# Reordering the first loads of a fused S5 + SwiGLU kernel: w1 of the first two gate tiles on both queues behind chunks 0 and 1 of x, chunk 3 of x behind w3

## The chip, the cores and the metric

The kernel runs on one core of a Trainium2 chip. Times are device microseconds (us) of that core, and the metric is the time of one execution. A "span" is the time from the first to the last instruction of a profiled execution; it is some 2 us shorter than the timed execution.

Engine names: PE is TensorE's matmuls, PEld its weight loads, DVE is VectorE, ACT is ScalarE, POOL is GpSimd, SP is SyncE. A q behind a name (SPq) is that engine's instruction sequencer.

## The reference

A layer norm of x (2048 tokens of 512 features) feeds a state-space layer (part A) and a SwiGLU block (part B). Both are added to x. Cut to what matters here:

```python
def _B_ref(x, w1, w3, w2):                      # w1, w3: 512 x 1792
    gate = jnp.einsum("bsd,df->bsf", x, w1)
    up = jnp.einsum("bsd,df->bsf", x, w3)
    h = _silu(gate) * up
    return jnp.einsum("bsf,fd->bsd", h, w2)

x = A_x
xn = _layernorm(x, axis=-1)
return x + _A_ref(xn, ...) + _B_ref(xn, B_w1, B_w3, B_w2)
```

## The kernel before

The kernel takes tokens in four blocks of 512, each of four chunks of 128. TensorE can begin its real work when chunk 0 of x has landed, been normalized and transposed, and the first columns of w1 have landed. The head of the program issues its first transfers for that; `nc.sync` and `nc.scalar` are the two engines that issue.

```python
    def load_w(f0, f1, eng1=nc.sync, eng3=nc.sync):
        eng1.dma_start(out=w1_sb[:, :, f0:f1], in_=w1v[:, :, f0:f1])
        eng3.dma_start(out=w3_sb[:, :, f0:f1], in_=w3v[:, :, f0:f1])

    for c in range(2):                      # chunks 0 and 1: a half on each queue
        for eng, dsl in ((nc.sync, slice(0, D // 2)), (nc.scalar, slice(D // 2, D))):
            eng.dma_start(out=x_blk[0][:, c, dsl], in_=xv[:, c, dsl])
    nc.scalar.dma_start(out=x_blk[0][:, 3, :], in_=xv[:, 3, :])
    nc.sync.dma_start(out=x_blk[0][:, 2, :], in_=xv[:, 2, :])
    load_w(0, 2 * P)                        # first w1, first w3: 256 KB each
    load_w(2 * P, 4 * P)                    # second w1, second w3
    # ... cut: bulk_loads() issues the rest, after a wait for ScalarE
```

The first weights are used here. `quarter` multiplies one chunk of tokens with some gate tiles, first with w1, then with w3:

```python
            def quarter(cl, fs, parts=1):
                tsl = slice(cl * P, (cl + 1) * P)
                n = NDT // parts
                for side, w in ((0, w1_sb), (1, w3_sb)):
                    for i in range(0, NDT, n):
                        for f in fs:
                            for dt in range(i, i + n):
                                nc.tensor.matmul(...)      # 128 columns
            # ... cut: chunks 0 and 1 are normalized and transposed
            ln_stats(0, 2)                  # VectorE: statistics of chunk 2
            ln_first_rstd(2)
            ln_stats(0, 3)                  # VectorE: statistics of chunk 3
            ln_first_rstd(3)
            ln_apply(0, 2)                  # VectorE: only now is chunk 2 normalized
            ln_apply(0, 3)
            quarter(0, (0, 1), 2)           # 8 matmuls with w1, then 8 with w3
            quarter(1, (0, 1))              # again, for chunk 1
            # ... cut
            ln_first_transpose(2)
            quarter(0, (2,))                # third tile: second w1, second w3
            ln_first_transpose(3)
```

Note the order on VectorE: chunk 2 is normalized after the statistics of chunk 3, so the transposes of chunk 2 wait for the landing of chunk 3.

Of the kernel before, what the change touches and what calls it, by code (L numbers as in the profile page):

```python
# [17 lines left out]
P = 128  # L18
# [45 lines left out]
def kernel(  # L64
# [17 lines left out]
    nc = tc.nc  # L82
# [26 lines left out]
    xv = A_x[0].rearrange("(c p) d -> p c d", p=P)  # L109
# [15 lines left out]
    w1_sb = const.tile([P, NDT, F], BF16, name="w1_sb")  # L125
    w3_sb = const.tile([P, NDT, F], BF16, name="w3_sb")
# [24 lines left out]
    x_blk = [x_all[:, i] for i in range(NBLK)]  # L151
    w1v = B_w1.rearrange("(t p) f -> p t f", p=P)
    w3v = B_w3.rearrange("(t p) f -> p t f", p=P)
# [4 lines that stand above are left out]
# [6 lines left out]
    for c in range(2):  # L164
        for eng, dsl in ((nc.sync, slice(0, D // 2)), (nc.scalar, slice(D // 2, D))):
            eng.dma_start(out=x_blk[0][:, c, dsl], in_=xv[:, c, dsl])
    nc.scalar.dma_start(out=x_blk[0][:, 3, :], in_=xv[:, 3, :])
    nc.sync.dma_start(out=x_blk[0][:, 2, :], in_=xv[:, 2, :])
    load_w(0, 2 * P)
    load_w(2 * P, 4 * P)  # L170

    def bulk_loads():
# [1111 lines left out]
```

## Time and profile before

| | before |
|---|---|
| timed runs, beside the changed kernel | 200.99, 200.81, 201.39, 201.04 us, median 201.01 |
| profiled span | 198.9 us |
| first w3: issued, landed | 2.59, 6.64 us |
| second w3: landed | 8.62 us |
| start of the last matmul to end of span | 2.98 us |

"Landed" is when the last of the 16 DMA engines that share a transfer has finished it. Read such a kernel as a full engine (TensorE) with a head in front of it and a tail behind: only a hole in TensorE's stream, a later start, or a longer tail moves the end. The prediction below shows the lines of the head (waits: who waits, for whom: us in all, times, longest).

```profile
SPq L1279 <- DMA out_dram<-xn: 1.0, 3, 0.5
```

```profile
196.53 0.36 ACTq L1072 DMA_DIRECT2D out_dram<-xn  x1
```

The last store is issued at 196.53, and the span ends 198.9 − 196.53 = 2.4 us later. In between SyncE waits three times for stores.

### The profile page before, as it was taken

The page shows a single profiled execution, that of the slowest core. Times are in us where ns is not written, and L with a number is a line of the kernel's source. Part 1 is how long each engine was busy: PE and PEld are TensorE (multiplying, and loading weights), DVE is VectorE, ACT ScalarE, POOL GpSimd, SP SyncE. Part 2 cuts the span into 40 slices and gives each one's busy share as a digit, 9 for nine tenths or more (in the row PEclk, how much of TensorE's full clock was granted, in tenths as well). Part 3 has the DMA queues.
Part 4 walks back from the last instruction along what each step waited for, and adds up shares of the span by engine and source line. Part 5 has one row for each costly group of instructions (what it writes and reads, how often), then busy time and mean ns, then how long its engine had stood idle before and what let it go on. Part 6 is the DMA issues. An engine that isn't in the chain of part 4 may idle for free.

```text
span 198.9 us, 3703 instructions
## 1 busy us (share of the span) xinstructions
PE 195.2 (98%) x1401; PEld 130.7 (66%) x1401; DVE 182.2 (92%) x257; ACT 135.0 (68%) x281; POOL 50.9 (26%) x75
## 2 busy tenths in 40 slices
PE   8999999999999999999999999999999999999994
PEld 2874444444444488856555478888566678888893
DVE  3699699999999999989999997999999999999972
ACT  4899797799999987968998684362688782111220
POOL 7170289700411134041202305040021303300000
PEclk9999999999999999999999999999999999999999
DMA  5999999992497054730997546838147723941111
GB/s 154 319 240 185 328 200 98 348 280 46 70 181 141 0 105 82 135 106 0 164 154 107 100 83 108 169 84 124 53 64 134 143 52 57 170 96 33 53 40 44
DMA packets 32258, 25.12 MB, mean 126 GB/s; under 512 B 16240, under 2 KB 29936, under 8 KB 32240
## 3 DMA queue, kind: packets, MB, share of 16 engines
q0 software_dynamic: 6128, 11.38, 33.6%
q1 hardware_dynamic: 25536, 13.21, 28.2%
q10 hardware_dynamic: 576, 0.30, 0.5%
q8 instruction: 11, 0.18, 0.4%
q14 instruction: 7, 0.06, 0.1%
HBM read 7.74 MB, written 2.10 MB: 49 GB/s over the span
## 4 chain that ended last, share of the span: by engine, by line
PE 96%; DMA 1%; DVE 1%; issue 0%
PE gu_ps L587 34%; PE gu_ps L1055 18%; PE y_ps L1055 10%; PE gu_ps L849 7%; PE bu_ps L1055 7%; PE y_ps L454 3%; PE bu_ps L454 3%; PE y_ps L870 3%; PE y_ps L781 3%; PE gu_ps L619 2%; PE gu_ps L781 2%; PE bu_ps L781 1%; PE bu_ps L870 1%; DMA x_blk<-in_A_x_dram 1%; PE bu_ps L619 1%; PE y_ps L243 1%
## 5 line engine op out<-in xcount | busy, mean ns | idle before, releaser
L587 PE MATMUL gu_ps<-xnT,w_sb 128*128 128x512 bf16 x312 | 69.6, 379 | 0.0
L587 PEld LDWEIGHTS <-w_sb 128*128 128x128 bf16 x312 | 30.5, 98 | 34.2
L1055 PEld LDWEIGHTS <-act 128*128 128x128 f16 x462 | 43.5, 98 | 5.4
L596 ACT ACTIVATE g<-gu_ps 128x512 bf16<-128x512 f32 x41 | 24.8, 606 | 5.9 <-PE gu_ps L587 3.5
L597 ACT ACTIVATE u<-gu_ps 128x512 bf16<-128x512 f32 x41 | 24.9, 606 | 4.4 <-PE gu_ps L587 4.1
L505 DVE TENSOR_TENSOR_SCAN u<-rho,ends,u 128x512 bf16<-128x512 f32 x16 | 20.0, 1271 | 0.0
L527 POOL DMA_DIRECT2D act<-p x7 | 9.2, 1321 | 34.1 <-DVE act L519 22.1
L1055 PE MATMUL gu_ps<-w_sb,act 128*128 128x256 bf16 (+3 forms) x126 | 16.0, 267 | 0.0
L849 PE MATMUL gu_ps<-xnT,w_sb 128*128 128x512 bf16 x64 | 15.9, 379 | 0.0
L604 DVE TENSOR_TENSOR act<-g,u 128x1024 f16<-128x1024 bf16 x21 | 14.3, 680 | 0.0
L861 ACT ACTIVATE g<-gu_ps 128x512 bf16<-128x512 f32 x14 | 8.4, 599 | 5.4 <-PE gu_ps L849 5.0
L454 PEld LDWEIGHTS <-bt 128*128 128x128 bf16 x64 | 6.3, 98 | 7.5
L1078 ACT ACTIVATE x_blk<-gu_ps 128x256 f32<-128x256 f32 (+1 forms) x9 | 3.3, 368 | 10.6 <-PE gu_ps L1055 10.6
L1055 PE MATMUL bu_ps<-w_sb,act 128*128 128x256 bf16 (+3 forms) x84 | 10.4, 264 | 0.0
L1055 PE MATMUL gu_ps<-ct,act 128*128 128x256 f16 (+1 forms) x72 | 10.4, 267 | 0.0
L849 PEld LDWEIGHTS <-w_sb 128*128 128x128 bf16 x64 | 6.3, 98 | 4.8
L505 DVE TENSOR_TENSOR_SCAN u<-rho,u 128x512 bf16<-128x512 f32 x8 | 9.2, 1207 | 0.0
L1055 PEld LDWEIGHTS <-x_blk 128*128 128x128 f16 x88 | 8.6, 98 | 1.0
L1055 PEld LDWEIGHTS <-tw 128*128 128x128 f16 x88 | 8.6, 98 | 1.0
L513 DVE TENSOR_TENSOR p<-u,tabe 128x2048 f16<-128x2048 bf16 (+1 forms) x8 | 8.7, 1086 | 0.1
L519 DVE TENSOR_TENSOR act<-u,tabe 128x2048 f16<-128x2048 bf16 (+1 forms) x8 | 8.7, 1085 | 0.0
L488 DVE TENSOR_TENSOR u<-u,tabe 128x2048 bf16<-128x2048 bf16 x7 | 8.5, 1220 | 0.1
(203 smaller groups left out, 392.5 us busy)
## 6 DMA issues: line engine op xcount, KB each, us to landing
act<-p POOLq DMA_DIRECT2D x6, 512.0 KB, 6.1
xn<-x_blk POOLq DMA_DIRECT2D x4, 512.0 KB, 5.5
out_dram<-xn SPq DMA_DIRECT2D x15, 128.0 KB, 1.7
w_sb<-in_B_w_dram SPq DMA_DIRECT2D x1, 1792.0 KB, 8.2
act<-act POOLq DMA_DIRECT2D x5, 352.0 KB, 4.6
w_sb<-in_B_w_dram SPq DMA_DIRECT2D x2, 768.0 KB, 6.1
u<-p POOLq DMA_DIRECT2D x3, 512.0 KB, 5.2
w_sb<-in_B_w_dram SPq DMA_DIRECT2D x4, 256.0 KB, 4.4
```

Of the source, the lines that this page charges most:

```text
L454: nc.tensor.matmul(out=ps, lhsT=bt[:, ri, dt, pt * P:(pt + 1) * P], rhs=xnT_blk[b][:, dt, :], start=(dt == 0), stop=(dt == NDT - 1))
L505: nc.vector.tensor_tensor_scan(out=v, data0=rho[:, pt:pt + 1].to_broadcast([P, TBLK]), data1=v, initial=init, op0=ALU.mult, op1=ALU.add)
L513: nc.vector.tensor_tensor(out=by_state(st["p16"][:, csl]), in0=by_chunk(st["g"][:, :, ::-1, tsl]), in1=by_chunk(tabe[:, psl, 2:0:-1, tsl]) ...
L519: nc.vector.tensor_tensor(out=by_state(act_state(b, hf)[:, csl]), in0=by_chunk(st["g"][:, :, :, tsl]), in1=by_chunk(tabe[:, psl, 0:1, tsl] ...
L527: gp.dma_start(out=a, in_=p16, accum_op=ALU.add)
L587: nc.tensor.matmul(out=ps[:, tsl], lhsT=w[:, dt, f * P:(f + 1) * P], rhs=xnT[:, dt, tsl], start=(dt == 0), stop=(dt == NDT - 1))
L596: nc.scalar.activation(out=g16[:, f % 2, :], in_=g_ps, func=ACT.Silu)
L597: nc.scalar.activation(out=u16[:, f % 2, :], in_=u_ps, func=ACT.Copy)
L604: nc.vector.tensor_tensor(out=act_gates(b, f - 1), in0=split(g16), in1=split(u16), op=ALU.mult)
L781: nc.tensor.matmul(out=out[:, h * TH:(h + 1) * TH], lhsT=left[:, h, k, :], rhs=right[:, k, :], start=(start and h == 0 and k == 0), stop=( ...
L849: nc.tensor.matmul(out=ps, lhsT=w[:, dt, f * P:(f + 1) * P], rhs=xnT[:, dt, :], start=(dt == 0), stop=(dt == NDT - 1))
L1055: nc.tensor.matmul(out=out, lhsT=left[:, k, :], rhs=right[k][:, cols], start=(start and k == 0), stop=(k == NK - 1), skip_group_check=True)
```

## The change

The intent: w1 of the first two gate tiles is wanted first, so half of it goes on each queue directly behind chunks 0 and 1 of x. Chunk 3 of x isn't wanted soon, so it goes behind w3.

```diff
-    nc.scalar.dma_start(out=x_blk[0][:, 3, :], in_=xv[:, 3, :])
+    for eng, k in ((nc.sync, 0), (nc.scalar, 2)):
+        eng.dma_start(out=w1_sb[:, k:k + 2, 0:2 * P], in_=w1v[:, k:k + 2, 0:2 * P])
     nc.sync.dma_start(out=x_blk[0][:, 2, :], in_=xv[:, 2, :])
-    load_w(0, 2 * P)
+    nc.sync.dma_start(out=w3_sb[:, :, 0:2 * P], in_=w3v[:, :, 0:2 * P])
+    nc.sync.dma_start(out=x_blk[0][:, 3, :], in_=xv[:, 3, :])
     load_w(2 * P, 4 * P)
```

Bytes are the same. The number of transfers rises by one, as w1 is now two.

## The prediction

> **What bounds the kernel now.** I read the page's first two parts first, to see whether there is an engine whose waits decide the end.
>
> ```profile
> PE 195.2 (98%) x1401; PEld 130.7 (66%) x1401; DVE 182.2 (92%) x257; ACT 135.0 (68%) x281; POOL 50.9 (26%) x75
> ...
> PE   8999999999999999999999999999999999999994
> ...
> DMA  5999999992497054730997546838147723941111
> ```
>
> TensorE (PE) is busy in every slice; only the first and the last are not full. The DMA engines are saturated in the first 40 us as well. So the end is the sum of the TensorE's work plus its few holes, and a change of loads can pay only through a hole. The list of waits for the TensorE has two entries, both before its real work:
>
> ```profile
> PE bu_ps L196 <- PEq L1268: 0.8, 1, 0.8
> PE y_ps L243 <- DVE xn L224: 0.2, 1, 0.2
> ```
>
> No wait for a weight is there, so I went on to the chain that ended last, in order of time, for the head (start, length, what):
>
> ```profile
> 0.73 2.39 DMA x_blk<-in_A_x_dram
> ...
> 3.14 0.70 DVE stats L219
> ...
> 6.32 1.88 PE gu_ps L619 x32
> 8.21 0.11 PE y_ps L315
> 8.31 0.33 PE y_ps L243 x4
> 8.64 0.45 PE bu_ps L619 x8
> ...
> 12.44 8.63 PE gu_ps L587 x40
> ```
>
> The head is: x chunk 0 lands (3.1 us), VectorE statistics, transposes, then the first gate tiles (L619, matmuls of 128 columns) from 6.2 us and no pause after. Eight of them take 0.45 us, 0.056 each. Thirty-two should take 1.79, and took 1.88: there is a hole of about 0.09 us in the first block, too small for the list of waits. The timeline of the weight loads (start, length, what) in three neighbouring windows finds it:
>
> ```profile
> 6.11 0.43 PEld L619 LDWEIGHTS <-w_sb 128*128 128x128 bf16 x7
> 6.44 0.15 PEld L619 LDWEIGHTS <-w_sb 128*128 128x128 bf16 x2
> 6.69 1.29 PEld L619 LDWEIGHTS <-w_sb 128*128 128x128 bf16 x23
> ```
>
> Loads 1 to 8 (the first two tiles' w1) run every 0.056 us from 6.11; the eighth starts at 6.50. The ninth, the first of w3, starts at 6.69 instead of 6.55. When did the transfers land? The timeline gives the issue, the view of one line's transfers the time to landing: w1 2.11 + 3.6 = 5.7; w3 2.59 + 4.1 = 6.7. So **w1 is 0.4 us early, w3 is what is late**, by 0.13 us at the load and, as matmul 9 could otherwise have started 0.056 after matmul 8 (6.55) and started at 6.69, by 0.08 us in the stream.
>
> The same reading for the third tile (f = 2), whose weights come with the next two transfers, issued 3.14 and 3.69, landing after 4.7 and 4.9: 7.8 and 8.6. The loads:
>
> ```profile
> 8.43 0.27 PEld L619 LDWEIGHTS <-w_sb 128*128 128x128 bf16 x4
> 8.67 0.14 PEld L619 LDWEIGHTS <-w_sb 128*128 128x128 bf16 x2
> ```
>
> Loads 1 to 4 (w1) start 8.43 to 8.59; the fifth (w3) would follow at 8.65, and came at 8.67. This second w3 transfer lands at the very moment when it is wanted. There is no slack behind it. After that, matmul starts follow one another by columns and clock to the end of the kernel; I found no other hole above 0.03 us.
>
> **What the Trainium skill says.** (1) "DMA: Bandwidth & Descriptors", section "Issuing engines are not separate DMA queues": transfers issued by ScalarE and SyncE run on the same 16 DMA engines, and spreading them saves only issue time. Here an issue takes 0.37 to 0.51 us on SyncE and the engines are over 100% busy from 4 to 12 us (windows view, DMA share 1.01 to 1.11), so the trace agrees: what counts is the bytes ahead of a transfer. (2) The same page, "Queues, rings and completion order": each DMA engine takes turns between the queues that have work, and a queue's descriptors are consumed in ring order. The landings of before (x 2 and 3 at 4.9 and 5.1, then 5.7, 6.7, 7.8, 8.6) are in order of issue, so I count bytes in issue order. (3) "TensorE: Matmul & The Clock Gate", "Wait — 56ns, not 53.3ns?": warm matmuls follow each other after columns / 2.4 GHz plus about 2.5 ns, 55.6 and 215.7 ns for 128 and 512 columns. The chain agrees: 8.63 / 40 = 0.216 us.
>
> **The change, part by part.** The order on TensorE, VectorE, ScalarE's compute and POOL is the same; only the loads move: ScalarE's queue gets half of w1 for chunk 3 of x, SyncE's gets half of w1, x 2, w3, x 3, and one issue more in all. No byte is added. Landings before, by cumulative KB: 512 at 5.1, 768 at 5.7, 1024 at 6.7, 1280 at 7.8, 1536 at 8.6. By those (an estimate):
>
> - w1, both halves, at 512 KB: 5.1 instead of 5.7. Wanted at 6.11. It had 0.4 us to spare; worth nothing.
> - x 2 at 640 KB: about 5.4 instead of 4.9. VectorE takes it at 5.78: hidden.
> - w3 at 896 KB: about 6.2 instead of 6.7. Wanted at 6.55: the hole closes, **-0.08 us**.
> - x 3 at 1024 KB: about 6.7 instead of 5.1. VectorE wanted it at 6.60, so the statistics of chunk 3 slip by 0.1 us, and with them both normalizations behind them (chunk 2's ends at 7.82 + 0.1, chunk 3's at 8.49 + 0.1). The transposes want them at 8.24 and 8.87, or 0.08 earlier if the hole closes: 0.24 and 0.2 us to spare. Hidden.
> - The loads of tiles 2 and 3: the extra issue pushes theirs from 3.14 and 3.69 to about 3.6 and 4.2, but the engines are a backlog of over 2 us behind by then (1024 KB issued by 3.6 land at 6.7), so landings stay at 7.8 and 8.6. TensorE now arrives 0.08 us earlier and waits for this second w3: **+0.08 us**.
> - SyncE is done with its issues by about 4.7; the next waits for ScalarE and went at 4.94 anyway.
>
> Sum: -0.08 + 0.08 = 0. The hole moves from the first w3 to the second. Even the whole hole is 0.04% of 201 us.
>
> **The rivals.** (a) *The second w3 lands early enough too*: then the 0.08 us stay, 200.9 us. For it: the landing at 8.6 is read only to 0.1 us, and w1 now shares two queues. Against: bytes ahead of it are the same. (b) *x 3 becomes the bound*: if it lands later than about 7.0, transposes of chunk 2, then the whole stream, wait one for one. For it: it goes from 1.5 us early to 0.1 us late. Against: it would have to be 0.3 us later than its bytes say; 0.3 us too late would give 201.2 to 201.3. (c) *The later issue of the second w3 shows*: its issue is 0.5 us later; if half of that reached the landing, TensorE would wait some 0.25 us, 201.2. Against: the saturated engines. (d) *Chunks 0 and 1 are slowed by the smaller pieces of w1 behind them* (512-byte rows in place of 1 KB): chunk 0 is the start of the chain, so each 0.1 us would count in full. Against: chunk 0 landed at 3.1, little more than 1 us after the next transfers were issued, and ring order puts them behind. (e) A gain above 0.2 us would need TensorE to start its gate tiles sooner, but the transposes ahead of them hang on x 0, VectorE and ScalarE, which the change leaves alone.
>
> **Range and chances.** I take 201.0, the median of before. The mechanisms move it by -0.1 to +0.3; the three runs of before spread from 200.81 to 201.39, so the scatter is as large. Range 200.6 to 201.5. Two per cent is 4 us, more than fifty times the hole: faster 0.01, within 0.98, slower 0.01.
>
> **What would show it right or wrong.** Right: in the changed profile the ninth L619-type weight load follows the eighth after 0.056 us; the first w3 lands near 6.2, x 3 near 6.7; the fifth load of the third tile then stands 0.1 us late, just after the second w3's landing at 8.6; the x512 stream starts at the same time as before (12.28) within 0.1. Wrong: a hole before the transposes of chunk 2 or 3 (rival b), the second w3 landing at 8.8 or later (c), chunk 0's statistics starting later than 3.14 (d), or a stream that starts by over 0.2 us sooner, which I have no source for.

## More of the kernel before

"L621" is a line of the kernel; a change in the head shifts the numbers by up to three lines, so L619 of the kernel before is L621 of the changed one.

From the start of the last matmul to the end of the span it is 2.98 us. Results of block 0 are held and stored later; the last stores of the last block are issued by SyncE and ScalarE, and the program then ends in instructions that the kernel doesn't write: waits for its transfers. The waits of SyncE's sequencer (who waits, for whom: us in all, times, longest) and the timeline (start, length, what) of the kernel before show both.

```python
    for cl, o in held:                      # 4 stores of 128 KB
        nc.sync.dma_start(out=ov[:, cl, :], in_=o)
```

## The result, and the profile after

The changed kernel takes 201.93 us (median; 201.83, 201.91, 202.40, 201.94), the kernel before 201.01 beside it. The ratio is 1.0048, with a 95% interval of 1.0026 to 1.0069. Ratios here are the mean time of one kernel's fast runs over that of the other's of the same rounds, so not quite the ratio of the medians quoted. The change is well within 2%, but it is a real loss of about 0.9 us, and 201.93 lies outside the range of 200.6 to 201.5.

The page of the changed kernel, its span, engine totals and the slices of TensorE and of the DMA engines:

```profile
span 200.1 us, 3704 instructions
...
PE 195.1 (98%) x1401; PEld 130.7 (65%) x1401; DVE 182.2 (91%) x257; ACT 134.9 (67%) x281; POOL 50.5 (25%) x75
...
PE   7899999999999999999999999999999999999993
...
DMA  5999999990498054730997446838147723940201
```

TensorE does the same work in the same time (195.1 against 195.2), with one digit less in the first slice and in the last. So the loss sits in the head and in the tail. The waits of TensorE have a new entry, for a weight:

```profile
PE bu_ps L198 <- PEq L1270: 0.8, 1, 0.8
PE gu_ps L621 <- DMA w_sb<-in_B_w_dram: 0.6, 1, 0.6
PE y_ps L245 <- DVE xn L226: 0.3, 1, 0.3
```

The timeline of the changed kernel (start, length, what; in brackets the idle time before and what ended it) places it:

```profile
5.96 0.49 PEld L621 LDWEIGHTS <-w_sb 128*128 128x128 bf16 x8
7.20 1.34 PEld L621 LDWEIGHTS <-w_sb 128*128 128x128 bf16 x24 [0.75 <-DMA w_sb<-in_B_w_dram]
7.62 0.69 DVE L221 BATCH_NORM_STATS2 stats<-x_blk 128x6 f32<-128x512 bf16 x1 [1.08 <-DMA x_blk<-in_A_x_dram]
```

The eight loads of w1 run from 5.96, some 0.15 us earlier than before. The ninth, the first of w3, comes at 7.20, after 0.75 us in which no weight was loaded, just after the first w3 has landed (7.16). VectorE's statistics of chunk 3 begin at 7.62, when chunk 3 has landed. The view of one line's transfers tells the way of the first w3 (issue time and, last, issue to landing), here before and then after:

```profile
L157 SPq DMA_DIRECT2D w_sb<-in_B_w_dram x1: 507/507/507, 2.6 to 2.6; - x1
...
DMA to landing us min/median/max: 4.1/4.1/4.1
```

```profile
L170 SPq DMA_DIRECT2D w_sb<-in_B_w_dram x1: 434/434/434, 2.6 to 2.6; - x1
...
DMA to landing us min/median/max: 4.5/4.5/4.5
```

It is issued at nearly the same time (2.62 instead of 2.59) with fewer bytes ahead of it, and lands 7.16 − 6.64 = 0.5 us later. The chain that ended last passes through chunk 3 of x in the changed kernel:

```profile
3.10 4.49 DMA x_blk<-in_A_x_dram
...
7.62 0.71 DVE stats L221
...
8.53 0.31 DVE xn L226
8.89 0.40 PE y_ps L245 x4
9.28 0.45 PE bu_ps L621 x8
...
13.12 8.63 PE gu_ps L589 x40
```

The stream of 512-column matmuls starts 13.12 − 12.44 = 0.68 us later than before. Step by step: the ninth load is 7.20 − 6.69 = 0.51 later than before; chunk 2's transposes, which wait for chunk 3's statistics to let VectorE go on, load at 8.88 instead of 8.24, which is 0.64 later; the rest, 0.04, comes behind. The 0.51 and the 0.64 are not a sum. The transposes follow chunk 3, as the chain shows, and would have stood at 8.88 even if the first w3 had landed in time. So in this profile the wait that ends last is that for chunk 3 of x, and the hole before w3 is hidden in front of it. With chunk 3 in time the late w3 would still have cost about the 0.51 by itself. The last matmul begins at 196.64 instead of 195.95, 0.69 later: nothing is lost or won between. Then the tail. The last store's issue in the timeline, and SyncE's waits, after:

```profile
197.22 0.36 ACTq L1074 DMA_DIRECT2D out_dram<-xn  x1
```

```profile
SPq L1281 <- DMA out_dram<-xn: 1.4, 1, 1.4
```

SyncE waits for stores once, for 1.4 us, instead of three times. From the start of the last matmul to the end it is now 3.42 instead of 2.98 us, 0.44 longer. Head 0.69 and tail 0.44 are 1.13 us, and the unrounded spans differ by 1.12. The profiled pair is thus accounted for in full; its head is above what the timed runs lose on the mean, as the experiments show.

### The profile page after: what moved, and what is told of

Read it like the earlier page. It is cut to its first block, busy times and chain, and to the rows that moved or that the text cites. A ratio compares the mean times of both kernels' runs of the same rounds, so it can differ in the third digit from the quotient of the medians.

```text
span 200.1 us, 3704 instructions
## 1 busy us (share of the span) xinstructions
PE 195.1 (98%) x1401; PEld 130.7 (65%) x1401; DVE 182.2 (91%) x257; ACT 134.9 (67%) x281; POOL 50.5 (25%) x75
## 4 chain that ended last, share of the span: by engine, by line
PE 94%; DMA 2%; SPq 1%; DVE 1%; issue 0%
PE gu_ps L589 34%; PE gu_ps L1057 17%; PE y_ps L1057 10%; PE gu_ps L851 7%; PE bu_ps L1057 7%; PE bu_ps L456 3%; PE y_ps L456 3%; PE y_ps L872 3%; PE y_ps L783 3%; DMA x_blk<-in_A_x_dram 2%; PE gu_ps L783 2%; PE bu_ps L783 1%; PE bu_ps L872 1%; PE bu_ps L621 1%; PE gu_ps L621 1%; SPq L166 0%
## 5 line engine op out<-in xcount | busy, mean ns | idle before, releaser
L221 DVE BATCH_NORM_STATS2 stats<-x_blk 128x6 f32<-128x512 bf16 x8 | 5.4, 681 | 4.1 <-DMA x_blk<-in_A_x_dram 4.1
```

## The experiments

Kernels of one call share a chip and the runs of the kernel before. All outputs were correct. Each diff is against the kernel before unless it says otherwise; where a run only writes `load_w(0, 2 * P)` out as its two transfers, or adds an `assert`, the diff shown leaves that out. A "hole" is the time without a weight load before the ninth load, and a "tail" the time from the start of the last matmul to the end of the span. At first I looked for the whole loss in the head. My theory was that w1 in two halves sets the 16 DMA engines apart, so that the w3 behind it waits for the slowest; rivals were the place of chunk 3 and later issues.

### First call: is it real, and which part?

**after_again**, the changed kernel unchanged:

> The changed kernel once more, to see whether its late w3 is of the order of loads or of one profile. Theory A (the new order makes one DMA engine fall behind in the first w3 transfer; three of four w1-split suspects are tested beside this run): w3 lands at 6.9 us or later, the TensorE hole before the ninth weight load is 0.5 us or more, time 201.7 to 202.2. Theory C (a slow engine of that one profile, the time difference has another cause): w3 lands at 6.2 to 6.6, no hole, and yet about 201.9.

Measured: 202.02 us beside 200.83, ratio 1.0051 [1.0027, 1.0076]. First w3 landed at 7.11. The timeline of the weight loads shows the same hole:

```profile
7.16 0.90 PEld L621 LDWEIGHTS <-w_sb 128*128 128x128 bf16 x16 [0.68 <-DMA w_sb<-in_B_w_dram]
```

The loss repeats.

**x3_behind**, only chunk 3 moved behind w3:

```diff
-    nc.scalar.dma_start(out=x_blk[0][:, 3, :], in_=xv[:, 3, :])
     nc.sync.dma_start(out=x_blk[0][:, 2, :], in_=xv[:, 2, :])
     load_w(0, 2 * P)
+    nc.sync.dma_start(out=x_blk[0][:, 3, :], in_=xv[:, 3, :])
```

> Chunk 3 of x behind w3 on the same queue, w1 whole and in its old place, nothing else. Theory A1 (splitting w1 over both queues sets the engines apart): w3 lands at 6.2 to 6.6, x 3 by 6.9, no hole above 0.1 us, time 200.9 to 201.1. Theory A2 (x 3 behind w3, so that SyncE's queue carries everything, is what costs): w3 at 6.9 or later or x 3 at 7.4 or later, hole 0.3 us or more in sum, time 201.5 to 202.0.

Measured: 201.14, ratio 1.0007 [0.9988, 1.0026]. First w3 landed at 6.51, without a hole before it:

```profile
6.06 1.83 PEld L620 LDWEIGHTS <-w_sb 128*128 128x128 bf16 x32
```

Chunk 3 landed at 7.28, and TensorE waited about 0.46 us for the normalized chunk 2 in the profile, as its list of waits says too:

```profile
PE y_ps L244 <- DVE xn L225: 0.4, 1, 0.4
```

The transposes of chunk 2 load at 8.56 instead of 8.24, and the last matmul begins at 196.35 instead of 195.95, with w3 in time: the late chunk 3 alone delays the stream in this profile. In time, this part alone can't be told from nothing. But the kernel before took 200.78 to 200.89 in five runs and 201.40 and 201.43 in two, and this one 201.05 to 201.25 in all four, so the mean of the kernel before holds slower executions of its own.

**w1_split**, only the halves of w1, chunk 3 where it was but behind ScalarE's half:

```diff
+    for eng, k in ((nc.sync, 0), (nc.scalar, 2)):
+        eng.dma_start(out=w1_sb[:, k:k + 2, 0:2 * P], in_=w1v[:, k:k + 2, 0:2 * P])
     nc.scalar.dma_start(out=x_blk[0][:, 3, :], in_=xv[:, 3, :])
     nc.sync.dma_start(out=x_blk[0][:, 2, :], in_=xv[:, 2, :])
-    load_w(0, 2 * P)
+    nc.sync.dma_start(out=w3_sb[:, :, 0:2 * P], in_=w3v[:, :, 0:2 * P])
```

> w1 of the first two tiles in halves on both queues, chunk 3 of x stays on ScalarE's queue behind its half, not behind w3. Theory A1 (the split sets the engines apart): w3 lands at 6.9 or later, hole 0.4 us or more, time 201.5 or more. Theory A2 (x 3 behind w3 costs): w3 about 6.5, x 3 about 5.6, time 200.9 to 201.1.

Measured: 202.25, ratio 1.0056 [1.0034, 1.0079]. In its profile chunk 0 landed some 0.5 us late and w3, the ninth transfer, was issued only at 3.61: it waits for the semaphore of an earlier transfer, a half of chunk 0, that landed at 3.59. It landed at 7.67.

**x3_ahead**, the changed kernel with chunk 3 ahead of w3 (diff against the changed kernel):

```diff
+    nc.sync.dma_start(out=x_blk[0][:, 3, :], in_=xv[:, 3, :])
     nc.sync.dma_start(out=w3_sb[:, :, 0:2 * P], in_=w3v[:, :, 0:2 * P])
-    nc.sync.dma_start(out=x_blk[0][:, 3, :], in_=xv[:, 3, :])
```

> The changed kernel with chunk 3 of x moved ahead of w3 on SyncE's queue, w1 still in halves on both. x 3 then has as many bytes ahead of it as in the kernel before plus w1. Theory A1 (the split): w3 is still late, 6.9 us or later, hole 0.4 or more, time 201.5 or more. Theory A2 (x 3 behind w3): x 3 lands near 5.7, w3 near 6.6, time 200.9 to 201.2.

Measured: 202.21, ratio 1.0058 [1.0036, 1.0081], with w3 landed at 7.31 and the second w3 at 10.25. What follows, as I read it then: the three kernels with halves of w1 lose 0.5%, the one without loses nothing, so the halves are the cause. That reading fell later. These three are also the ones with one transfer more.

### Second call: the halves, or the place?

**w1_whole**, the changed kernel's order without halves, all on SyncE:

```diff
-    nc.scalar.dma_start(out=x_blk[0][:, 3, :], in_=xv[:, 3, :])
+    nc.sync.dma_start(out=w1_sb[:, :, 0:2 * P], in_=w1v[:, :, 0:2 * P])
     nc.sync.dma_start(out=x_blk[0][:, 2, :], in_=xv[:, 2, :])
-    load_w(0, 2 * P)
+    nc.sync.dma_start(out=w3_sb[:, :, 0:2 * P], in_=w3v[:, :, 0:2 * P])
+    nc.sync.dma_start(out=x_blk[0][:, 3, :], in_=xv[:, 3, :])
```

> The changed order with w1 as one transfer on SyncE's queue right behind the first chunks, then x 2, w3, x 3; ScalarE's queue carries only its halves of chunks 0 and 1. If cutting w1 in two over both queues is what delays w3: w3 lands 6.3 to 6.6, no hole before the ninth weight load above 0.1 us, x 3 near 7.2 as with x 3 behind w3 alone, time 201.0 to 201.3. If it is the place of w1 ahead of x 2: w3 7.0 or later, hole 0.5, time 201.7 or more.

Measured: 201.42 beside 200.95, ratio 1.0030 [1.0010, 1.0050]. First w3 landed at 6.75, hole 0.20 us, chunk 3 at 7.16, tail 2.98. So the order costs something without any halves.

**halves_sync**, the changed kernel with both halves on SyncE (diff against the changed kernel):

```diff
-    for eng, k in ((nc.sync, 0), (nc.scalar, 2)):
-        eng.dma_start(out=w1_sb[:, k:k + 2, 0:2 * P], in_=w1v[:, k:k + 2, 0:2 * P])
+    for k in (0, 2):
+        nc.sync.dma_start(out=w1_sb[:, k:k + 2, 0:2 * P], in_=w1v[:, k:k + 2, 0:2 * P])
```

> As the run with w1 whole, but w1 as two half transfers one after the other on SyncE's queue. If the second queue is what sets the DMA engines apart: w3 lands by 6.7, time 201.0 to 201.3, as with w1 whole. If the cut into smaller transfers alone does it: w3 at 7.0 or later, hole 0.4 or more, time 201.6 or more.

Measured: 202.09, ratio 1.0061 [1.0045, 1.0076], w3 landed at 7.35, hole 0.61. The loss needs no second queue.

**x_act**, chunks 2 and 3 both on ScalarE's queue, w1 and w3 whole on SyncE's:

```diff
+    nc.scalar.dma_start(out=x_blk[0][:, 2, :], in_=xv[:, 2, :])
     nc.scalar.dma_start(out=x_blk[0][:, 3, :], in_=xv[:, 3, :])
-    nc.sync.dma_start(out=x_blk[0][:, 2, :], in_=xv[:, 2, :])
     load_w(0, 2 * P)
```

> A try at a version better than both: chunks 2 and 3 of x on ScalarE's queue, w1 and w3 whole on SyncE's, so both queues carry the same bytes. If bytes ahead decide and queues take turns: w3 lands at 6.3 to 6.7, x 2 near 5, x 3 near 5.6, no hole above 0.1 us, time 200.7 to 201.0. If weights on one queue beside x on the other also set the engines apart: w3 at 7.0 or later and time 201.5 or more.

Measured: 201.49, ratio 1.0027 [1.0012, 1.0042]. Here w3 was issued at 2.12, 0.47 earlier than before, and still landed at 7.15. Issue time alone doesn't set the landing. In this profile TensorE's 128-column matmuls also ran at 0.107 us each until about 6.2, as in those of x3_ahead and after_5, so its head isn't a clean comparison.

**before_again**, one look at the kernel before:

> A second profile of the kernel before, to see how far its landings repeat. If the order sets them: w3 6.5 to 6.8, the second w3 8.4 to 8.8, hole before the ninth weight load under 0.2 us. If landings of single runs scatter by half a microsecond: w3 anywhere from 6.3 to 7.2.

Measured: one run, 201.42 beside a median of 200.95. In this second profile of the kernel before, the timeline of the weight loads has a hole as well:

```profile
7.31 0.78 PEld L619 LDWEIGHTS <-w_sb 128*128 128x128 bf16 x14 [0.85 <-DMA w_sb<-in_B_w_dram]
```

Its first w3 landed at 7.27 and its second at 8.87; chunk 3 landed early (4.73). Its last matmul begins 0.62 us later than in the first profile of the same kernel, with the same tail. So the profile that the prediction was read from showed a good execution (200.71 us); the kernel before has bad ones too, and the 0.69 us of head between the two profiles first compared are hardly more than these 0.62.

### Third call: later issue, cut alone, another queue

**late_issue**, the kernel before with a transfer of 128 bytes on SyncE ahead of w3:

```diff
-    load_w(0, 2 * P)
+    nc.sync.dma_start(out=w1_sb[:, :, 0:2 * P], in_=w1v[:, :, 0:2 * P])
+    dummy = const.tile([1, 64], BF16, name="dummy")
+    nc.sync.dma_start(out=dummy, in_=A_Dskip[0:64].rearrange("(o d) -> o d", o=1))
+    nc.sync.dma_start(out=w3_sb[:, :, 0:2 * P], in_=w3v[:, :, 0:2 * P])
```

> The kernel before with one tiny transfer (128 bytes) put ahead of w3 on SyncE's queue: no bytes added to speak of, but w3 and all later loads are issued about 0.5 us later. If bytes ahead decide (my prediction): w3 still by 6.6 to 7.0, time 200.9 to 201.1. If the landing follows the issue: w3 at 7.0 to 7.2, second w3 at 9.0 to 9.2, time 201.4 to 201.8.

Measured: 202.07 beside 201.06, ratio 1.0049 [1.0027, 1.0072]: the whole loss of the change, with its bytes and its order left as before. w3 was issued at 3.03 and landed at 7.36. In this profile chunk 1 was late as well (4.30 instead of 3.46), so the later issue is not all that differs in its head.

**cut_in_place**, the kernel before with w1 as two halves, in its place and on its queue:

```diff
-    load_w(0, 2 * P)
+    for k in (0, 2):
+        nc.sync.dma_start(out=w1_sb[:, k:k + 2, 0:2 * P], in_=w1v[:, k:k + 2, 0:2 * P])
+    nc.sync.dma_start(out=w3_sb[:, :, 0:2 * P], in_=w3v[:, :, 0:2 * P])
```

> The kernel before with only w1 cut into two half transfers, both on SyncE's queue in w1's old place. w3 is issued 0.5 us later, as with the tiny transfer. If later issue is all that a cut costs: the same time as that run within 0.3 us (201.4 to 201.8). If the cut itself sets the engines apart: 201.9 or more and a last engine over 1 us behind the median one in w3. If neither: 201.0.

Measured: 202.48, ratio 1.0077 [1.0056, 1.0098]; w3 issued at 3.10, landed at 8.03, 1.09 us after its 8th DMA engine. This is what was expected if the cut itself sets the engines apart. All four runs (202.41 to 202.68) lie above the four of late_issue (201.47 to 202.22), which has as many transfers and issues w3 at nearly the same time. So the halves seem to cost something in this place beyond the extra transfer, though the two intervals overlap; why isn't shown.

**w1_act**, w1 whole on ScalarE's queue behind chunks 0 and 1, chunk 3 behind w3:

```diff
-    nc.scalar.dma_start(out=x_blk[0][:, 3, :], in_=xv[:, 3, :])
+    nc.scalar.dma_start(out=w1_sb[:, :, 0:2 * P], in_=w1v[:, :, 0:2 * P])
     nc.sync.dma_start(out=x_blk[0][:, 2, :], in_=xv[:, 2, :])
-    load_w(0, 2 * P)
+    nc.sync.dma_start(out=w3_sb[:, :, 0:2 * P], in_=w3v[:, :, 0:2 * P])
+    nc.sync.dma_start(out=x_blk[0][:, 3, :], in_=xv[:, 3, :])
```

> The changed kernel with w1 whole on ScalarE's queue: w3 is issued near 2.1 us with fewer transfers ahead of it on its own queue. If issue time decides: w3 lands 6.2 to 6.6, second w3 near 8.7, time 200.8 to 201.1, the best so far. If two queues with weights set the engines apart: w3 at 7.0 or later, 201.5 or more.

Measured: 200.59, ratio 0.9986 [0.9967, 1.0006]. w3 was issued at 2.11 and landed at 6.12, no hole before it:

```profile
6.04 1.83 PEld L620 LDWEIGHTS <-w_sb 128*128 128x128 bf16 x32
```

**par_first_after**, the changed kernel with GpSimd's three small loads of parameters issued earlier:

```diff
+    for i, src in enumerate((A_log_dt, A_Lambda_re, A_Lambda_im)):
+        nc.gpsimd.dma_start(out=par_rows[i * NPT:(i + 1) * NPT, :], in_=src.rearrange("(t p) -> t p", p=P))
     nc.gpsimd.memset(eps_t, LN_EPS)
     # ... and the same loop, further down, taken out
```

> The changed kernel with the three tiny parameter loads of POOL issued 0.8 us earlier, ahead of its fills, so that they are done before w3 is under way. If these loads, whose completions fall at 5.1 to 6.5 us beside w3, hold up single DMA engines: w3 lands by 6.6, time 201.0 to 201.2. If they have no part in it: w3 7.0 to 7.3 and 201.7 to 202.2 as in the changed kernel.

Measured: 202.09, ratio 1.0055 [1.0033, 1.0078], w3 landed at 7.51. The small loads had all landed by 5.19 (6.49 in the changed kernel), before the first DMA engine was done with w3 (5.54), so they aren't what delays w3 here.

Laid side by side, the times from the start of the last matmul to the end of the span fell into two groups, which no theory of the head explains: 3.40 to 3.43 in every kernel with eleven transfers in the head (the changed one, w1_split, x3_ahead, halves_sync, late_issue, cut_in_place, par_first_after), and 2.97 to 2.99 in every one with ten. The records of the last instructions tell why. SyncE ends the program with nine waits in a row, always in the same order and about 0.062 us apart if none has to wait; eight of them, the second to the ninth, hold one each of the eight semaphores of the transfers. The transfers of SyncE and ScalarE take these semaphores in rotation. Which of them the last store has depends on how many transfers went before it. The view of the wait line in a window at the end shows it (count, durations in ns, first and last start). The kernel before, 197.50 to 198.08, and the changed one, 198.7 to 199.2:

```profile
L1279 SPq EVENT_SEMAPHORE  x3: 28/28/28, 197.5 to 198.0; - x3
```

```profile
L1281 SPq EVENT_SEMAPHORE  x8: 27/28/28, 198.7 to 199.2; - x8
```

Before, the waits end as the last three stores land one after another, and the last store's semaphore is the eighth and last of these. In the changed kernel it is the first of the eight: SyncE stands there until the last store lands, and all eight then go through in a row. Seven more at 0.062 us are 0.43 us, after the last byte.

### Fourth call: the tail and the head apart

**merged_split**, halves of w1 on both queues as in the changed kernel, but chunks 2 and 3 of x as one transfer, so that the count stays at ten:

```diff
-    nc.scalar.dma_start(out=x_blk[0][:, 3, :], in_=xv[:, 3, :])
-    nc.sync.dma_start(out=x_blk[0][:, 2, :], in_=xv[:, 2, :])
-    load_w(0, 2 * P)
+    for eng, k in ((nc.sync, 0), (nc.scalar, 2)):
+        eng.dma_start(out=w1_sb[:, k:k + 2, 0:2 * P], in_=w1v[:, k:k + 2, 0:2 * P])
+    nc.sync.dma_start(out=x_blk[0][:, 2:4, :], in_=xv[:, 2:4, :])
+    nc.sync.dma_start(out=w3_sb[:, :, 0:2 * P], in_=w3v[:, :, 0:2 * P])
```

> The changed kernel with chunks 2 and 3 of x as one transfer (so w1 is still in halves on both queues, but ten transfers instead of eleven go ahead of the big loads, and the second w1 and w3 are issued 0.5 us earlier). Theory N (one transfer more than before in the head, wherever it stands, costs the microsecond; a cut of w1 costs only through it): w3 by 6.7, time 200.7 to 201.2. Theory H (halves of w1 themselves set the engines apart): w3 at 7.0 or later, 201.7 or more.

Measured: 201.51 beside 201.18, ratio 1.0010 [0.9990, 1.0030], tail 2.99. With halves but no extra transfer the loss is not seen. The theory of the halves falls as an account of the whole 0.5%. Two limits: chunk 3 is no longer behind w3 here either, and the interval, up to 0.6 us, would still hide a cost of the halves as large as the head's share. In the profile w3 landed at 7.52, a hole of 0.64, with chunk 1 itself late (4.25).

**dummy_behind**, the kernel before with a transfer of 128 bytes behind all loads of the head:

```diff
     load_w(2 * P, 4 * P)
+    dummy = const.tile([1, 64], BF16, name="dummy")
+    nc.sync.dma_start(out=dummy, in_=A_Dskip[0:64].rearrange("(o d) -> o d", o=1))
```

> The kernel before with the tiny transfer put behind the second w3, so that no load that TensorE waits for is issued later. Theory I (later issue is what costs): as before, 200.8 to 201.2, w3 near 6.6. Theory N (the mere number of transfers): 201.7 to 202.2 as with the tiny transfer ahead of w3.

Measured: 201.69, ratio 1.0030 [1.0014, 1.0045]: a transfer of 128 bytes that nobody reads, and that stands behind everything in the head, costs 0.3%. 0.003 of 201 is 0.6 us, in agreement with 0.44 for the tail. Its tail is 3.40, and its waits of SyncE are the changed kernel's:

```profile
SPq L1282 <- DMA out_dram<-xn: 1.4, 1, 1.4
```

late_issue has the same tiny transfer ahead of w3, and 1.0049: the later issue of w3 and what follows points to some 0.4 us more, though the intervals overlap.

**w1_act_merged**, w1 on ScalarE's queue and chunks 2 and 3 as one transfer, nine in the head:

```diff
-    nc.scalar.dma_start(out=x_blk[0][:, 3, :], in_=xv[:, 3, :])
-    nc.sync.dma_start(out=x_blk[0][:, 2, :], in_=xv[:, 2, :])
-    load_w(0, 2 * P)
+    nc.scalar.dma_start(out=w1_sb[:, :, 0:2 * P], in_=w1v[:, :, 0:2 * P])
+    nc.sync.dma_start(out=x_blk[0][:, 2:4, :], in_=xv[:, 2:4, :])
+    nc.sync.dma_start(out=w3_sb[:, :, 0:2 * P], in_=w3v[:, :, 0:2 * P])
```

> The version with w1 whole on ScalarE's queue, and chunks 2 and 3 of x as one transfer ahead of w3: nine transfers. If fewer and earlier issues help further: w3 by 6.5 (1 us of bytes more ahead than with x 3 behind), the loads of the third tile 0.4 us earlier, time 200.4 to 200.7. If that version was already without a hole: 200.5 to 200.7, no gain.

Measured: 201.04, ratio 0.9999 [0.9986, 1.0011]; w3 landed at 6.83, no gain from fewer issues. Its tail is 3.04. One transfer fewer makes the last store's semaphore the seventh, and one wait of 0.06 follows: the rotation again.

**w1_act_5**, w1_act again in five rounds:

> The version with w1 whole on ScalarE's queue again, in five rounds, to see whether it beats the kernel before. If its missing hole is real: 200.5 to 200.8 and a ratio of 0.998 to 0.999 with an interval below 1. If its first four runs were lucky: ratio 0.999 to 1.001.

Measured: 201.09, ratio 0.9997 [0.9985, 1.0010]. In its profile w3 landed at 6.60, and chunk 3 at 7.13 instead of 6.68 in the third call. The gain of the third call is not there. No version beats the kernel before reliably.

### Fifth call: the changed kernel without its tail

**after_tail**, the changed kernel with two of the stores held from block 0 made into one, so that the program's count of transfers is that of before (diff against the changed kernel):

```diff
-    for cl, o in held:
+    for cl, o in held[:2]:
         nc.sync.dma_start(out=ov[:, cl, :], in_=o)
+    nc.sync.dma_start(out=ov[:, 2:4, :], in_=xn_blk[0][:, 2:4, :])
```

> The changed kernel with two stores of finished rows in mid-kernel merged into one, so that the whole kernel has as many transfers as before; the head is untouched. In the profiles so far the end comes 2.98 us after the last matmul's start where the kernel has as many transfers as before, and 3.42 us where it has one more: SyncE ends the program by waiting for eight completion semaphores in turn, 0.063 us each, and the last store's stands last with the old number and second with one more. Theory T (0.44 us of the loss is this tail): 2.98 us again, time 201.3 to 201.6, 0.4 below the changed kernel in the same rounds. Theory D (all of the loss is in the head): time as the changed kernel within 0.15.

**after_5**, the changed kernel in five rounds beside it:

> The changed kernel once more in five rounds beside it, on the same chip: 201.7 to 202.1 in both theories; the difference to the run with the merged store is what is asked: 0.4 us for theory T, under 0.15 for theory D.

Measured: after_tail 201.40, ratio 1.0025 [1.0003, 1.0046]; after_5 201.94, ratio 1.0044 [1.0030, 1.0059]; the kernel before 201.11. The edit far from the head took 201.94 − 201.40 = 0.54 us off the median and 0.47 off the mean. The six runs of after_tail spread from 201.13 to 202.35, so the timed difference alone is barely clear of noise; the profile is the sharper witness. Its tail is 2.99 against 3.42 in after_5, and SyncE's waits, with 1.4 us in one wait in after_5, are again those of before:

```profile
SPq L1283 <- DMA out_dram<-xn: 1.0, 3, 0.5
```

The head of after_tail is the changed kernel's, with the hole:

```profile
7.02 1.06 PEld L621 LDWEIGHTS <-w_sb 128*128 128x128 bf16 x19 [0.67 <-DMA w_sb<-in_B_w_dram]
```

What is left of the loss, 0.0025 × 201 = 0.5 us, with an interval of 0.06 to 0.9, is the head's. w1_whole, the same order with no halves and no extra transfer, gives 1.0030, the same within the intervals.

### The head, engine by engine

A transfer is shared by 16 DMA engines. The trace records when each of them is done. For the first w3, and beside it the landing of chunk 3 of x and the first load of chunk 2's transposes (us):

| kernel (one profile each) | w3 issued | 8th of 16 done | last done | chunk 3 landed | transposes of chunk 2 | ratio in time |
|---|---|---|---|---|---|---|
| before | 2.59 | 6.40 | 6.64 | 5.11 | 8.24 | – |
| before_again | 2.59 | 6.21 | 7.27 | 4.73 | 8.87 | – |
| after | 2.62 | 5.87 | 7.16 | 7.60 | 8.88 | 1.0048 |
| after_again | 2.62 | 5.79 | 7.11 | 7.48 | 8.77 | 1.0051 |
| after_5 | 2.71 | 5.96 | 7.47 | 7.88 | 9.17 | 1.0044 |
| after_tail | 2.62 | 5.92 | 6.98 | 7.39 | 8.68 | 1.0025 |
| w1_whole | 2.66 | 5.90 | 6.75 | 7.16 | 8.45 | 1.0030 |
| x3_behind | 2.59 | 5.94 | 6.51 | 7.28 | 8.56 | 1.0007 |
| w1_act | 2.11 | 5.87 | 6.12 | 6.68 | 8.08 | 0.9986 |

The last columns settle which of the two late loads holds the stream in a profile. In all six from after to x3_behind the transposes come 1.28 or 1.29 us after chunk 3 has landed, whenever w3 did: chunk 3 is what they wait for. In before_again chunk 3 was early and the late w3 alone delayed them. Either load is enough, and with the changed order both are late together. In w1_act neither was late, and its transposes came the earliest.

In the changed kernel the 8th engine is done with w3 half a microsecond earlier than before, as fewer bytes ahead suggest, and 13 of 16 are by 5.97. The last takes until 7.16, and TensorE's ninth load starts only then. The engines as a whole are not full in that time. The view of windows (us, busy time and count of TensorE, of its weight loads, VectorE, ScalarE and GpSimd, then granted clock, DMA share, GB/s), before and then after:

```profile
6.00:6.50 0.50, 0.50 (x11) 0.50 (x12) 0.47 (x1) 0.27 (x2) 0.00 (x0) 1.00 1.07 321
6.50:7.00 0.50, 0.50 (x11) 0.41 (x9) 0.49 (x2) 0.50 (x2) 0.00 (x0) 1.00 1.15 331
```

```profile
6.00:6.50 0.50, 0.50 (x12) 0.45 (x9) 0.47 (x2) 0.29 (x1) 0.00 (x0) 1.00 0.69 177
6.50:7.00 0.50, 0.12 (x3) 0.00 (x0) 0.04 (x1) 0.49 (x2) 0.00 (x0) 1.00 1.06 290
```

Between 6.0 and 6.5 the share falls to 0.69 and the rate from 321 to 177 GB/s, while a part of w3 is still on its way. TensorE's matmuls then stand still in the second window (0.12 of 0.50). The Trainium skill, "DMA: Bandwidth & Descriptors", section "Why a DMA increments its semaphore by 16 and not by 1", says that a DMA runs on up to 16 SDMA engines that finish independently, and that only the full count of 16 means that all data landed. The trace agrees: it is the last engine's 7.16, not the middle one's 5.87, that TensorE's ninth load follows, at 7.20.

## Why the prediction was wrong, point by point

**The failed step that the trace shows in full: the tail.** The prediction counted "and one issue more in all. No byte is added." and followed it only so far: "SyncE is done with its issues by about 4.7; the next waits for ScalarE and went at 4.94 anyway." At SyncE's next wait the extra issue indeed did not matter (the issue behind it went at 4.79 instead of 4.94). It shifts the last store to another of eight semaphores, and the program's end takes 3.42 instead of 2.98 us. That is 0.44 us of a term that the sum didn't have. It is shown by taking it away (after_tail, 2.99) and by adding it alone (dummy_behind, 3.40). With the tail taken away the changed kernel took 201.40, inside the range of 200.6 to 201.5.

**The failed step of the head: x 3 "at 1024 KB: about 6.7 instead of 5.1 ... Hidden."** It landed at 7.60, 0.9 us later than that. The step counted 0.24 us to spare, and the statistics of chunk 3 slipped by 1.02 us instead of 0.1 (7.62 instead of 6.60). So rival (b), "transposes of chunk 2, then the whole stream, wait one for one" if x 3 lands later than about 7.0, came true in all four profiles of the changed order: 7.60 is 0.6 later than 7.0, and the transposes stood 0.64 later. The mechanism of (b) was right, and the landing was mis-sized. In timed runs x3_behind, this move alone, is 1.0007, not told from nothing; its profile shows the wait.

**The second failed step of the head: "the hole closes, -0.08 us".** The working behind it, w3 "at 896 KB: about 6.2 instead of 6.7", is near the 8th DMA engine, which was done at 5.87. It fails for the landing, 7.16. I took landings of before, read one profile, and interpolated by bytes, as if all 16 engines were in step. In the trace of before that was nearly so (6.40 and 6.64); a second look at the same kernel had 6.21 and 7.27. In place of −0.08 the changed order has a hole of 0.67 to 0.75 us in four profiles. In those it lies in front of the wait for chunk 3, so it adds nothing of its own there. Both together are worth some 0.5 us (interval 0.06 to 0.9) in timed runs of after_tail, where the kernel before also pays at times.

**"so landings stay at 7.8 and 8.6": wrong.** The second w1 and w3 landed at 8.2 to 8.8 and 9.1 to 9.7 in the profiles of the changed order, issued half a microsecond later. Rival (c), which the prediction set aside for "the saturated engines", named this sign (8.8 or later), but before_again had 8.12 and 8.87 without any later issue, so the cause isn't shown. It did not become a hole of its own in the profile after: TensorE was already late.

**Right.** w1 "had 0.4 us to spare; worth nothing": its halves landed at 4.67 and 4.92, and TensorE could not start on them before 5.96. x 2 was hidden (landed at 5.25). Chunk 0 wasn't slowed in the profile after, its statistics started at 2.99, so rival (d) fell there (in w1_split's profile it was late, 3.62). TensorE's total stayed. The class, within 2%, was right and was given 0.98.

**What stays open.** Why single DMA engines fall about 1 us behind in the first w3, and in chunk 3 behind it, isn't settled. It happens with all of w1 on one queue (halves_sync) and with GpSimd's small loads out of the way (par_first_after), and an earlier issue does not prevent it (x_act). It occurs in the kernel before as well, so the head's share isn't cleanly separated from scatter that the new order may only make more frequent. Whether the halves add to it is open too: merged_split shows no cost, cut_in_place does. No run keeps w1 in halves on both queues with both the first w3 and chunk 3 in time.

## What to carry to other kernels

Follow a change in the number of transfers to the very end of the program: the last store's place among the semaphores that are waited for there can be worth almost half a microsecond, whatever the transfer itself does, and it can be tested by a tiny transfer that nobody reads. Take a load's landing from its slowest DMA engine in more than one profile; here an estimate by cumulative bytes (6.2) was nearer to the middle engine (5.87) than to the last (7.16). When two waits stand in a row, ask of the later one whether it would have stood there without the first: here it would, so closing the first hole alone would have won nothing in these profiles. When every kernel of a group loses the same, look for what else they share besides the part that you changed, before you call that part the cause.

## What the Trainium skill lacked or had wrong

- No page has the waits at the program's end: eight semaphores in turn, 0.062 us apart, used in rotation by the transfers. The end took 3.40 to 3.43 us from the start of the last matmul where the last store's semaphore was the first of the eight, and 2.97 to 2.99 where it was the last.
- "DMA: Bandwidth & Descriptors", section "Why a DMA increments its semaphore by 16 and not by 1", says that the engines finish independently but not how far apart. On the same 256 KB load, the first w3, the last was behind the eighth by 0.24 us in one profile of the kernel before, by 1.06 in another, and by 1.3 in the changed kernel.
